# One set of the fifth group's first dense product as seven block products, with its casts moved

## The chip, the cores and the metric

The kernel runs on one core of a Trainium2 chip. The metric is the device time of one execution in microseconds (us), as the median of several runs. TensorE (PE) does matrix products and accumulates them in PSUM, a memory of banks that VectorE (DVE) and ScalarE (ACT) read. DVE, ACT and GpSimd (POOL) do the elementwise work, and SyncE (SP) issues the transfers. Each engine works through its own instructions in order and waits for others by semaphores.

## The reference

Two operators in a row: an attention with decay over blocks of 64 tokens, and a dense layer, gelu and dense layer on its result.

```python
for b in range(nb):                         # blocks of 64 tokens, 4 batches, 8 heads, 768 tokens, 64 wide
    intra = (qb @ kb^T * Dmask) @ vb        # inside the block
    inter = (qb * lam_pow) @ kv_state       # from all blocks before
    out[:, :, sl] = intra + inter
    kv_state = lam_block * kv_state + (kb * rev_pow)^T @ vb
x = out as 3072 tokens x 512
h = x @ w_in                                # 512 -> 2048, the first dense product
g = 0.5 * h * (1 + tanh(c * (h + 0.044715 * h**3)))
y = g @ w_out                               # 2048 -> 512
```

The types on the chip are float16 for the factors and float32 for the sums.

## The kernel before

The attention goes in 24 steps (0 to 23): 256 tokens of one batch, four of the eight heads. For each step the query is scaled and cast by DVE, the key cast by ACT, the value scaled by POOL, and query and key are transposed by a DMA:

```python
def cast_qk(s):
    q32, k32, _ = ld32[s]
    tqk = a16p.tile([P, 2, 2, HH, D], FP16, tag="qk16", name=f"qk16_{s}")
    tq, tk = tqk[:, 0], tqk[:, 1]
    q_eng = nc.gpsimd if s == 3 else nc.vector
    pin(q_eng.tensor_tensor(wide(tq), q32[:], decay(dq, s), ALU.mult))
    ...
    pin(nc.scalar.activation(out=wide(tk), in_=k32[:], func=AF.Copy))
```

The loaded q32, k32 and v32 lie in pools of four buffers each. Two steps' attention products are issued together as a "burst": four banks for the scores S, two for O, two for K, out of one pool of eight PSUM banks:

```python
def burst(ns, ss, *mix):
    for n in ns:
        scores(n)                                        # S: 2 banks each
    O = [ps_M.tile(..., name=f"O{c}") for c in range(2)]
    ...                                                  # O += PT x v
    if ns:
        K = [ps_M.tile(..., name=f"K{c}") for c in range(2)]
    ...                                                  # K = k^T v, then O += u x q
    for n in ns:
        causal(n)                                        # DVE: PT = S * mask, frees S
    for i, s in enumerate(ss):
        x_out(s, ...)                                    # ACT: O to xT
    ...
    for n in ns:
        update(n, 0)                                     # DVE, POOL: state from K
```

The dense layers go by groups of steps; a group's matmuls are small pieces in a queue, from which `fill(n)` takes n. In groups 0 to 4 the first product is made of pieces `mm1` (four matmuls of 512 columns, then a gelu by ACT):

```python
groups = [[0, 1], [2], [3], [4, 5], [6, 7], [8, 9], [10, 11]]
def mm1(fs):
    Hps = ps_M.tile([P, per, N], FP32, tag="M", name="Hps")
    for i, f in enumerate(fs):
        for c in range(NC):
            pin(nc.tensor.matmul(by_block(Hps[:, i, :]), w_in16[:, c, f * P : (f + 1) * P],
                                 x(c), start=(c == 0), stop=(c == NC - 1)))
    ...
    pin(nc.scalar.activation(out=dst, in_=Hps[:], func=AF.Gelu_apprx_tanh))
```

In groups 5 and 6 (`SEVEN`) it is done by Strassen-Winograd's seven products of 2x2 blocks in place of eight: four sums of x blocks (`sum_x`, tile xs) and four sums of weight blocks (`sum_win`, tiles ws), and for each set k the products m = 1 to 7, each four matmuls of 256 columns, accumulated in three banks HX, HW and HY:

```python
def seven(m, k):
    ...
    if m == 1:
        copied("m1", "q32", nc.scalar)      # ACT copies HX to a buffer of the q32 pool
    elif m == 2:
        added(0, 0, "m1")                   # DVE: m1 += HW, then a gelu by ACT
    elif m == 5:
        copied("q", "q32", nc.scalar)       # ACT copies HY
        release()                           # issues the gelus that are pending
    elif m == 6:
        copied("u2", "k32", nc.vector)      # DVE copies HX to a buffer of the k32 pool
    elif m == 3:
        added(0, 1, "u2")                   # DVE: u2 += HY
    elif m == 7:
        added(1, 1, "q")                    # DVE: q += HX
    elif m == 4:
        pending.insert(0, lambda: gelu(1, 0, dst[:]))
    if k == HF // 2 - 1 and m in (3, 7, 4):
        release()
```

m6, m7 and m4 accumulate on HX behind m1, and m3 on HY behind m5. The second dense product (banks MX, MW, MY) is done by seven block products in all groups but the first; `behind(k, ...)` attaches its DVE sums over gelu results (`sum_g`, tile gs) to the k-th piece of the group. The part of the program in question:

```python
    R(17, 15)                                # queues group 4
    fill(1); U(17); fill(1)
    sum_win(3, 0, nc.vector); fill(2)
    prep(19)
    sum_win(3, 1, nc.vector); fill(2)
    sum_win(4, 0, nc.vector); fill(2)
    sum_win(4, 1, nc.vector); fill(2)
    prep_qk(20); fill(1)
    prep_qk(21); prep_v(20); fill(3)
    burst((18, 19), (16, 17))
    prep_v(21); fill(2)
    U(18); U(19); fill(4)
    prep_qk(22); fill(2)
    burst((20, 21), (18, 19), 11, 4)         # queues group 5
    ...
```

Of the kernel before, what the change touches and what calls it, by code (L numbers as in the profile page):

```python
# [15 lines left out]
def kernel(  # L16
# [10 lines left out]
    nc = tc.nc  # L27
# [116 lines left out]
    def sum_win(m, j, eng):  # L144

        if not wi_sum:
            wi_sum.extend(wst.tile([P, 2, 2, DFF // 2], FP16, tag=f"w{2 + i}", name=f"ws{i}")
                          for i in range(2))
        a, op, b = I_SUMS[m]
        cs, fs = slice(0, 2), slice(512 * j, 512 * j + 512)  # L150
        pin(eng.tensor_tensor(w_in_block(m, cs, fs), w_in_block(a, cs, fs),
                              w_in_block(b, cs, fs), op))
# [17 lines left out]
    def load_ahead(s):  # L170
        if s < NSTEP:
            load_step(s)
# [76 lines left out]
    def wide(t):  # L249
        return t.rearrange("p j h d -> p h j d")  # L250

    def decay(t, s):
        hs = halves[s % 2]
        return t[:, hs, :].unsqueeze(3).to_broadcast([P, HH, 2, D])

    def prep_v(s):
        scale_v(s)
        if s >= 6:
            if s + 3 == FIRST_DMA_T + 1:
                load_step(s + 3, "qk")  # L260
            else:
                load_ahead(s + 3)
# [6 lines left out]
    def prep_qk(s):  # L269
        cast_qk(s)  # L270
        transpose_dma(s)

    def cast_qk(s):
        q32, k32, _ = ld32[s]
        tqk = a16p.tile([P, 2, 2, HH, D], FP16, tag="qk16", name=f"qk16_{s}")
        tq, tk = tqk[:, 0], tqk[:, 1]
        q_eng = nc.gpsimd if s == 3 else nc.vector
        pin(q_eng.tensor_tensor(wide(tq), q32[:], decay(dq, s), ALU.mult))  # L278
        if s == 0:
            inverse(halves[0])  # L280
            odd(halves[1])
            inverse(halves[1])
        pin(nc.scalar.activation(out=wide(tk), in_=k32[:], func=AF.Copy))  # L283
        a16[s] = (tq, tk)
        whole_qk[s] = tqk

    whole_qk = {}

    def transpose_dma(s):
        tqk = whole_qk.pop(s)  # L290
        if s >= FIRST_DMA_T:
            o = qkp.tile([P, 2, 2, 2, P], FP16, tag="qkT", name=f"qkT_{s}")
            pin(nc.sync.dma_start_transpose(out=o[:].rearrange("p a j h t -> p (a j h) t"),
                                            in_=tqk[:].rearrange("p a j h d -> p (a j h d)")))
            qkT[s] = o
            if s == FIRST_DMA_T:
                load_step(s + 1, "v")
# [219 lines left out]
        return gs_kept[1:]  # L517

    SEVEN = (5, 6)
    SLOTS = {5: {1: 0, 2: 1, 5: 1, 6: 1, 3: 1, 7: 1}, 4: {1: 0, 2: 1, 5: 0, 6: 1, 3: 1, 7: 1}}  # L520
    groups = [[0, 1], [2], [3], [4, 5], [6, 7], [8, 9], [10, 11]]
    group_of = {sb: (g, i) for g, sbs in enumerate(groups) for i, sb in enumerate(sbs)}
# [2 lines left out]
    def queue_group(g, lead=0, per_set=0):  # L525
# [69 lines left out]
        def product(m, p, part=None):  # L595

            st = of_group

            def bank(name):
                if name not in st:  # L600
                    st[name] = ps_M.tile([P, 1 if name == "X" else NP, HE], FP32, tag="M",
                                         name="M" + name[0])
                return st[name]

            if m in (2, 5, 3):
                dst = bank("Y" if m in (5, 3) else "W")[:, p]
            else:
                dst = bank(f"X{p}")[:, 0]
            opens = m == 1 or (m in (2, 5) and p == 0)
            closes = m in (2, 3, 4)  # L610
            a, b = FACTORS[m]
            for i in range(HF) if part is None else range(HF // 2 * part, HF // 2 * part + HF // 2):
                lhsT = g_rows(a, i)[:, p * P : p * P + P]
                if b in W_SUMS:
                    rhs = w_sum16[:, w_slot[b], i, :]
                else:
                    F, E = b
                    rhs = w_out16[:, F * HF + i, E * HE : E * HE + HE]
                pin(nc.tensor.matmul(dst, lhsT, rhs, start=(opens and i == 0),  # L619
                                     stop=(closes and i == HF - 1), skip_group_check=True))  # L620
            if part == 0:
                return
            last = p == NP - 1

            def temp(name):
                if name not in st:
                    st[name] = mtp.tile([P, NP, HE], FP32, tag=name, name=name)
                return st[name]

            def out_tile(T):  # L630
                if f"o{T}" not in st:
                    st[f"o{T}"] = otp.tile([P, NP, 2, HE], FP32, tag="o32", name=f"o{T}")
                return st[f"o{T}"]

            def copy(to, of):
                pin(nc.scalar.activation(out=to, in_=of, func=AF.Copy))  # L636

            def store(T, ps=slice(0, NP), es=slice(0, 2)):
                r = row0 + T * HN
                rows = out[r : r + HN, :].rearrange("(p q) (e d) -> q p e d", q=P, e=2)  # L640
                whole = g == 3
                for i in [ps] if whole else [slice(i, i + 1) for i in range(ps.start, ps.stop)]:
                    pin(nc.sync.dma_start(out=rows[:, i, es], in_=out_tile(T)[:, i, es, :]))

            one = slice(p, p + 1)
            if m == 1:
                copy(temp("m1")[:, p], dst)
            elif m == 2 and last:
                pin(nc.vector.tensor_tensor(out_tile(0)[:, :, 0, :], st["W"][:], st["m1"][:], ALU.add))
            elif m == 5 and last:  # L650
                copy(temp("q")[:], st["Y"][:])
            elif m == 6:
                copy(temp("u2")[:, p], dst)
            elif m == 3 and last:
                pin(nc.vector.tensor_tensor(out_tile(0)[:, :, 1, :], st["Y"][:], st["u2"][:], ALU.add))
                store(0)
            elif m == 7 and last_group:
                pin(nc.vector.tensor_tensor(out_tile(1)[:, p, 1, :], dst, st["q"][:, p], ALU.add))
                if last:
                    store(1, one, slice(1, 2))  # L660
            elif m == 7:
                copy(temp("u3")[:, p], dst)
                if last:
                    pin(nc.gpsimd.tensor_tensor(out_tile(1)[:, :, 1, :], st["u3"][:], st["q"][:],  # L664
                                                ALU.add))
            elif m == 4:
                copy(out_tile(1)[:, p, 0, :], dst)
                if last_group:
                    store(1, one, slice(0, 1 if last else 2))
                elif last:  # L670
                    store(1)
# [26 lines left out]
        def seven(m, k):  # L698
# [48 lines left out]
                added(1, 1, "q")  # L747
            elif m == 4:
                pending.insert(0, lambda: gelu(1, 0, dst[:]))
            if k == HF // 2 - 1 and m in (3, 7, 4):  # L750
                release()

        def merge(lead, per_set):
# [71 lines left out]
        def behind(k, i0, i1, ms):  # L825

            piece = filler[at + k]

            def both():
                piece()  # L830
                sum_g(i0, i1, ms)

            filler[at + k] = both
# [3 lines left out]
        if g in SEVEN:  # L837
# [6 lines left out]
            for k, m in enumerate((2, 4, 3)):  # L844
                behind(len(parts) * k, 4, 8, (m,))
            return
        for i in range(HF):
            for fs in ([[i, i + HF]] if per == 2 else [[i], [i + HF]]):
                filler.append(lambda fs=fs: mm1(fs))
        for m, p in order:  # L850
# [4 lines left out]
        if per == 2:  # L855
            behind(5, 0, 4, (1, 2))
            behind(6, 0, 4, (4, 3))
            behind(7, 4, 8, (1,))
            behind(8, 4, 8, (2,))
            behind(9, 4, 8, (4,))  # L860
            behind(10, 4, 8, (3,))
        else:
            behind(9, 0, 4, (1, 2) if g == 3 else (1, 2, 4, 3))
            if g == 3:
                behind(12, 0, 4, (4, 3))
            w = 2 if g + 1 in SEVEN else 1
            for k, m in zip((0, 3, 7, 11) if w == 2 else (0, 1, 2, 4), (1, 2, 4, 3)):
                behind(n1 + k, 4, 8, (m,))

    def fill(n):  # L870
        for _ in range(min(n, len(filler))):
            filler.pop(0)()
# [162 lines left out]
    U(17)  # L1035
    fill(1)
    sum_win(3, 0, nc.vector)
    fill(2)
    prep(19)
    sum_win(3, 1, nc.vector)  # L1040
    fill(2)
    sum_win(4, 0, nc.vector)
    fill(2)
    sum_win(4, 1, nc.vector)
    fill(2)
    prep_qk(20)
    fill(1)
    prep_qk(21)
    prep_v(20)
    fill(3)  # L1050

    burst((18, 19), (16, 17))
    prep_v(21)
    fill(2)
    U(18)
    U(19)
    fill(4)
    prep_qk(22)
    fill(2)
    burst((20, 21), (18, 19), 11, 4)  # L1060
    fill(3)
    U(20)
    U(21)
    fill(20)
    prep_qk(23)
    fill(23)
    prep_v(22)
    prep_v(23)
    fill(13)
# [34 lines left out]
```

## Time and profile before

| | |
|---|---|
| time, median of 3 runs | 199.9 us (199.7 to 201.04) |
| span of the profiled execution | 198.0 us |
| all first products Hps, 288 matmuls (L542) | 50.8 us |
| block products HX, HW, HY of groups 5 and 6, one matmul | 272 to 273 ns by the page |
| query cast on DVE, 23 times | 19.7 us, mean 859 ns |
| key cast on ACT, 24 times | 15.0 us, mean 626 ns |
| ACT waiting for Hps before its gelu | 8.8 us in 32 waits |
| POOL waiting for ACT's u before the addition o | 37.9 us in 5 waits |

The mean of a matmul on the page includes its way through the pipeline, so that neighbours overlap; how long a run of matmuls holds PE is better read from the chain of waits, where each piece is counted from the end of the one before. "Idle before" on an engine that is not on that chain costs nothing by itself. A line such as L542 is a line of the kernel before.

### The profile page before, as it was taken

Reading aid. Unit: us, or ns where it says so; the run is one execution under the profiler, and the core shown is the slowest. Engines: PE = TensorE matmul, PEld = TensorE weight load, DVE = VectorE, ACT = ScalarE, POOL = GpSimd, SP = SyncE. Lnnn points to the kernel's source line nnn. Section 1 sums busy time; section 2 is a strip of 40 time slices with the busy share of each in tenths; the row PEclk is TensorE's granted clock in tenths of the full one; section 3 lists DMA queues with packets and bytes.
Section 4 is the critical chain, followed back from the end, with each engine's and each line's share of the span. In section 5 each row is a group of like instructions: output and inputs, shape, how many; then the busy total and the mean of one; then the engine's idle time right before and its main releaser. Section 6 shows DMA issues by size and latency. Waiting matters only on the chain.

```text
span 198.0 us, 5937 instructions
## 1 busy us (share of the span) xinstructions
PE 191.6 (97%) x2439; PEld 140.2 (71%) x2439; DVE 153.9 (78%) x296; ACT 123.0 (62%) x251; POOL 75.5 (38%) x85
## 2 busy tenths in 40 slices
PE   8979999999999999999999999999999999999993
PEld 2546544456888888754588854578888888888882
DVE  4887722789999989969999927998778996588620
ACT  3673878457794675677645377844768836779221
POOL 6594213457557642465563526156002030002000
DMA  6999999999999999989994997400211200030205
GB/s 168 291 323 386 386 387 387 293 289 301 336 263 265 218 307 226 194 252 190 295 205 95 272 316 182 104 16 0 53 66 43 104 10 0 0 107 2 106 14 201
DMA packets 61722, 37.86 MB, mean 191 GB/s; under 512 B 17536, under 2 KB 54656, under 8 KB 61696
## 3 DMA queue, kind: packets, MB, share of 16 engines
q1 hardware_dynamic: 61152, 37.23, 72.9%
q8 instruction: 19, 0.31, 0.7%
q10 hardware_dynamic: 544, 0.26, 0.5%
q14 instruction: 7, 0.06, 0.1%
HBM read 27.26 MB, written 6.29 MB: 169 GB/s over the span
## 4 chain that ended last, share of the span: by engine, by line
PE 88%; SPq 4%; DMA 4%; ACT 1%; issue 1%
PE Hps L542 24%; PE MX L619 17%; PE MY L619 9%; PE HX L711 7%; PE O2ps L557 7%; PE MW L619 4%; DMA wi<-in_moe_w_in_dram 4%; SPq L70 4%; PE HY L711 4%; PE S L340 3%; PE Hps L802 3%; PE HW L711 2%; PE OK L398 2%; PE O L449 1%; PE O L424 1%; PE Tps L311 1%
## 5 line engine op out<-in xcount | busy, mean ns | idle before, releaser
L542 PE MATMUL Hps<-xT,w_in 128*128 128x512 f16 (+1 forms) x288 | 50.8, 332 | 0.0
L501 POOL TENSOR_TENSOR u<-t,lumask 128x256 f16<-128x256 f32 x40 | 31.0, 789 | 46.5 <-DVE t L494 28.4
L542 PEld LDWEIGHTS <-w_in 128*128 128x128 f16 x288 | 27.8, 98 | 19.0
L546 ACT ACTIVATE gT<-Hps 128x512 f16<-128x512 f32 x56 | 33.1, 598 | 9.3 <-PE Hps L542 8.8
L350 DVE TENSOR_TENSOR PT<-S,mask 128x512 f16<-128x512 f32 x48 | 30.3, 681 | 6.5 <-PE S L340 6.4
L619 PEld LDWEIGHTS <-gs 128*128 128x128 f16 x320 | 31.2, 98 | 3.6
L266 POOL TENSOR_TENSOR v<-v,dv 128x512 f16<-128x512 f32 x24 | 30.0, 1254 | 7.4 <-DMA v<-in_v_dram 7.2
L619 PEld LDWEIGHTS <-gT 128*128 128x128 f16 x240 | 23.2, 98 | 3.6 <-ACT gT L546 0.5
L619 PE MATMUL MX<-w_sum,gs 128*128 128x256 f16 x160 | 21.4, 273 | 0.0
L664 POOL TENSOR_TENSOR o<-u,q 128x512 f32<-128x512 f32 (+1 forms) x5 | 5.8, 1158 | 37.9 <-ACT u L636 37.9
L278 DVE TENSOR_TENSOR qk<-q,dq 128x512 f16<-128x512 f32 x23 | 19.7, 859 | 0.6 <-DMA q<-in_q_dram 0.5
L283 ACT ACTIVATE qk<-k 128x512 f16<-128x512 f32 x24 | 15.0, 626 | 6.5 <-DMA k<-in_k_dram 6.4
L589 DVE TENSOR_TENSOR gs<-gT 128x1024 f16<-128x1024 f16 (+1 forms) x24 | 17.6, 737 | 1.5 <-ACT gT L546 1.5
L557 PE MATMUL O2ps<-w_out,gT 128*128 128x512 f16 x64 | 14.6, 379 | 0.0
L475 ACT ACTIVATE xT<-OK 128x256 f16<-128x256 f32 x26 | 10.0, 453 | 7.3 <-PE OK L398 7.1
L711 PEld LDWEIGHTS <-ws 128*128 128x128 f16 x128 | 12.5, 98 | 1.8
L636 ACT ACTIVATE u<-MX 128x256 f32<-128x256 f32 x18 | 6.9, 384 | 10.2 <-PE MX L619 10.2
L475 ACT ACTIVATE xT<-O 128x256 f16<-128x256 f32 x22 | 8.0, 459 | 5.9 <-PE O L449 5.0
L557 PEld LDWEIGHTS <-gT 128*128 128x128 f16 x64 | 6.1, 98 | 6.6
L619 PE MATMUL MY<-w_out,gs 128*128 128x256 f16 x80 | 10.7, 273 | 0.0
L340 PEld LDWEIGHTS <-qkT 64*64 64x64 f16 x384 | 6.0, 106 | 6.5 <-issue 2.5
L589 DVE TENSOR_TENSOR gs<-gs,gT 128x1024 f16<-128x1024 f16 (+1 forms) x12 | 10.2, 851 | 0.3
(95 smaller groups left out, 319.4 us busy)
## 6 DMA issues: line engine op xcount, KB each, us to landing
q<-in_q_dram SPq DMA_DIRECT2D x24, 256.0 KB, 5.0
k<-in_k_dram SPq DMA_DIRECT2D x24, 256.0 KB, 5.2
v<-in_v_dram SPq DMA_DIRECT2D x23, 256.0 KB, 5.4
out_dram<-o SPq DMA_DIRECT2D x19, 256.0 KB, 4.3
wo<-in_moe_w_out_dram SPq DMA_DIRECT2D x4, 1024.0 KB, 9.5
wi<-in_moe_w_in_dram SPq DMA_DIRECT2D x4, 512.0 KB, 7.0
wi<-in_moe_w_in_dram SPq DMA_DIRECT2D x2, 1024.0 KB, 12.8
out_dram<-o SPq DMA_DIRECT2D x2, 512.0 KB, 6.6
```

The lines of the kernel that those rows point to most:

```text
L266: pin(nc.gpsimd.tensor_tensor(wide(tv[:]), ld32[s][2][:], decay(dv, s), ALU.mult))
L278: pin(q_eng.tensor_tensor(wide(tq), q32[:], decay(dq, s), ALU.mult))
L283: pin(nc.scalar.activation(out=wide(tk), in_=k32[:], func=AF.Copy))
L350: pin(nc.vector.tensor_tensor(t[:, hl].rearrange("p b c d -> p b (c d)"), Sps[:].rearrange("p b c d -> p b (c d)"), mask[:].unsqueeze(1).t ...
L475: pin(nc.scalar.activation(out=d, in_=o, func=AF.Copy))
L501: pin(nc.gpsimd.tensor_tensor(u[:], state[half][:].unsqueeze(2).to_broadcast([P, 2, 2, D]), lumask[:, 2 * half : 2 * half + 2, :].unsqueez ...
L542: pin(nc.tensor.matmul(by_block(Hps[:, i, :]), w_in16[:, c, f * P : (f + 1) * P], x(c), start=(c == 0), stop=(c == NC - 1)))
L546: pin(nc.scalar.activation(out=dst, in_=Hps[:], func=AF.Gelu_apprx_tanh))
L557: pin(nc.tensor.matmul(O2[tau][0][:], gT[:, f % HF, f // HF, tau * P : (tau + 1) * P], w_out16[:, f, :], start=(n == 0), stop=(n == NF - 1)))
L589: pin(nc.vector.tensor_tensor(g_rows(m, i), g_rows(a, i), g_rows(b, i), op))
L619: pin(nc.tensor.matmul(dst, lhsT, rhs, start=(opens and i == 0), stop=(closes and i == HF - 1), skip_group_check=True))
L711: pin(nc.tensor.matmul(dst[:, i, :], w_in_block(a, slice(c, c + 1), slice(f * P, f * P + P))[:, 0], x_block(b, slice(c, c + 1))[:, 0], sta ...
```

## The change

Group 4, the fifth, gets one of its sets (k = 0: rows 0, 1, 8 and 9 of sixteen) by the seven block products; the other twelve pieces stay as they were. It is meant to take matmul columns off PE: seven products of 4 x 256 columns for four pieces of 4 x 512. The group's four x sums are made ahead of it. Because the products' temporaries take buffers of the q32 and k32 pools, which here still carry loaded steps, the key casts of 20 and 21 are issued earlier, the load of 23 comes after the burst, and the casts of 22 and 23 come within the sixth group. The group's second store is issued in two halves.

```diff
+    def cast_q(s):
+        both16(s)
+        q_eng = nc.gpsimd if s == 3 else nc.vector
+        pin(q_eng.tensor_tensor(wide(a16[s][0]), ld32[s][0][:], decay(dq, s), ALU.mult))
+
+    def cast_k(s):
+        both16(s)
+        pin(nc.scalar.activation(out=wide(a16[s][1]), in_=ld32[s][1][:], func=AF.Copy))
...
+    MIXED = 4
...
-                whole = g == 3
+                whole = g == 3 and T == 0
...
-            if k == HF // 2 - 1 and m in (3, 7, 4):
+            if (k == HF // 2 - 1 or g == MIXED) and m in (3, 7, 4):
                 release()
...
-        for i in range(HF):
+        if g == MIXED:
+            sum_xs.append(sum_x)
+            plain = [[f] for i in range(2, HF) for f in (i, i + HF)]
+            for m in (1, 2, 5, 0, 6, 3, 0, 7, 0, 4):
+                filler.append((lambda m=m: seven(m, 0)) if m else (lambda fs=plain.pop(0): mm1(fs)))
+            for fs in plain:
+                filler.append(lambda fs=fs: mm1(fs))
+        for i in range(HF) if g != MIXED else ():
...
-            behind(9, 0, 4, (1, 2) if g == 3 else (1, 2, 4, 3))
+            n1 += 3 * (g == MIXED)
+            behind(n1 - 7, 0, 4, (1, 2) if g == 3 else (1, 2, 4, 3))
...
     sum_win(3, 0, nc.vector)
+    cast_k(20)
     fill(2)
     prep(19)
...
     fill(2)
+    cast_k(21)
     sum_win(4, 1, nc.vector)
-    fill(2)
-    prep_qk(20)
-    fill(1)
-    prep_qk(21)
-    prep_v(20)
+    for m in (1, 2, 3, 4):
+        sum_xs[0](m)
+    cast_q(20)
+    transpose_dma(20)
+    scale_v(20)
     fill(3)
+    cast_q(21)
+    fill(7)

     burst((18, 19), (16, 17))
+    transpose_dma(21)
+    load_ahead(23)
     prep_v(21)
-    fill(2)
+    fill(3)
     U(18)
     U(19)
-    fill(4)
-    prep_qk(22)
-    fill(2)
+    fill(3)
     burst((20, 21), (18, 19), 11, 4)
     fill(3)
     U(20)
     U(21)
     fill(20)
+    prep_qk(22)
+    fill(12)
     prep_qk(23)
-    fill(23)
+    fill(11)
     prep_v(22)
```

More of the change, by code (lines that the diff above doesn't have):

```diff
@@ L273, in cast_qk @@
     def cast_qk(s):
[L274 to L278, printed above, removed]
+        cast_q(s)
         if s == 0:
@@ L282, in cast_qk, with both16 @@
             inverse(halves[1])
-        pin(nc.scalar.activation(out=wide(tk), in_=k32[:], func=AF.Copy))
-        a16[s] = (tq, tk)
-        whole_qk[s] = tqk
+        cast_k(s)
+    def both16(s):
+        if s in a16:
+            return
+        tqk = a16p.tile([P, 2, 2, HH, D], FP16, tag="qk16", name=f"qk16_{s}")
+        a16[s] = (tqk[:, 0], tqk[:, 1])
+        whole_qk[s] = tqk
+    def cast_q(s):
[5 more added lines that the diff above has]
+        pin(nc.scalar.activation(out=wide(a16[s][1]), in_=ld32[s][1][:], func=AF.Copy))
     whole_qk = {}
@@ L519 @@
     SEVEN = (5, 6)
+    MIXED = 4
+    sum_xs = []
     SLOTS = {5: {1: 0, 2: 1, 5: 1, 6: 1, 3: 1, 7: 1}, 4: {1: 0, 2: 1, 5: 0, 6: 1, 3: 1, 7: 1}}
```

## The prediction

> **What bounds the kernel now.** I read the busy shares first, then the chain that ended last, then the order of time on each engine around 113 us, where the changed piece runs. The page's first line of numbers and the chain's share by engine:
>
> ```profile
> PE 191.6 (97%) x2439; PEld 140.2 (71%) x2439; DVE 153.9 (78%) x296; ACT 123.0 (62%) x251; POOL 75.5 (38%) x85
> PE 88%; SPq 4%; DMA 4%; ACT 1%; issue 1%
> ```
>
> TensorE (PE) is busy nearly always and carries 88% of the chain; the rest of it is the first loads and the last store. So a matmul cycle saved shortens the run, and any wait PE is made to take lengthens it: nothing later has slack to take it back. The chain in order of time (start, us, what), around the fifth group (steps 12 to 15, group 4 in the code) and in the sixth group's first set:
>
> ```profile
> 112.95 4.32 PE Hps L542 x20
> 117.26 0.57 PE S L340 x32
> 119.09 6.91 PE Hps L542 x32
> 125.99 0.57 PE S L340 x32
> ...
> 136.32 0.44 PE HY L711 x4
> 136.76 0.44 PE HX L711 x4
> 137.19 0.44 PE MX L619 x4
> 137.63 0.52 PE HY L711 x4
> ```
>
> Four 512-column matmuls take 4.32 / 5 = 0.864 us (one Hps piece); four of 256 columns take 0.437 us. The 0.52 of the last line is a 0.08 us wait: HY must wait until ScalarE has copied that bank. The copy ran 136.91 to 137.50, so PE restarts about 0.2 us after the end of the record it waits for. I use that 0.2 below.
>
> Now VectorE (DVE), GpSimd (POOL) and ScalarE (ACT) in order of time at the start of the group (start, us, engine, instruction, idle before):
>
> ```profile
> 111.70 2.35 DVE L278 TENSOR_TENSOR qk<-q,dq 128x512 f16<-128x512 f32 x2
> 117.66 2.48 DVE L350 TENSOR_TENSOR PT<-S,mask 128x512 f16<-128x512 f32 x4 [3.60 <-PE S L340]
> ...
> 111.70 1.81 POOL L664 TENSOR_TENSOR o<-u,q 128x512 f32<-128x512 f32 x1 [2.27 <-ACT u L636]
> 113.47 1.49 POOL L266 TENSOR_TENSOR v<-v,dv 128x512 f16<-128x512 f32 x1
> ...
> 112.98 0.38 ACT L636 ACTIVATE o<-MX 128x256 f32<-128x256 f32 x1 [0.49 <-PE MX L619]
> 113.85 0.60 ACT L546 ACTIVATE gT<-Hps 128x512 f16<-128x512 f32 x1 [0.48 <-PE Hps L542]
> ```
>
> DVE does the query casts of 20 and 21, then idles 3.6 us. The change puts its additions into that hole. But the two casts took 2.35 us where one elsewhere takes 0.68, and just then POOL has two operations.
>
> **What the Trainium skill says.** "SBUF — State Buffer", section "SBUF: two separate sides": a VectorE operation with two SBUF inputs and a GpSimd operation that reads SBUF share a port pair, as an exclusive lock held for the whole instruction. The trace agrees: the first cast ran 111.70 to 112.38; the second is recorded as 112.30 to 114.05 (1.75 us), ending 0.54 after POOL's o addition (111.70 to 113.51), and POOL's v scaling (113.47, 1.49 us) ends 0.9 us after that cast. Where nothing stands against them, the same o addition takes 1.27 (at 151.35) and the v scaling 1.04 (at 121.56). They take turns, one instruction each; 107 to 110 us shows the same turns. "TensorE: Matmul & The Clock Gate", "Back-to-back issue gap", gives 518 cycles for 512 columns and 262 for 256, that is, hardly any fixed cost for halving a matmul; 0.864 against 0.437 agrees. "PSUM — Partial Sum Buffer", "PSUM: the matmul accumulator": eight banks. All eight are in one pool here, and a burst takes eight (four S, two O, two K).
>
> **The change part by part.**
> *Matmul work.* Of the 16 Hps pieces four go (4 x 0.864 = 3.46 us); seven block products come (7 x 0.437 = 3.06). PE: **-0.40 us**. This is all that can be gained directly.
>
> *The schedule if nothing waits*, from 112.95, products by their number m: m1 to 113.39, m2 113.82, m5 114.26, Hps 115.13, m6 115.57, m3 116.00, Hps 116.87, m7 117.31, Hps 118.18, then the burst; m4 after it.
>
> *Wait A, m3.* m3 accumulates on the bank of m5, so ACT must first have copied it (0.60). That copy's buffer is the fourth-oldest of the query buffers, the one of step 20, so it waits for the query cast of 20 on DVE. Ahead of that cast now stand the four x sums, each with two SBUF inputs. DVE ends its weight sums at 111.78 as before. In turns with POOL: first x sum to 112.1, POOL o (1.27) to 113.35, second x sum to 113.7, POOL v (1.04) to 114.7, third and fourth x sum (0.34 apart without contention, at 163.16 and 163.50) to 115.4, cast (0.6) to 116.0. ACT copy to 116.65, PE at 116.85 instead of 115.57: **+1.28 us**. Were there no turns, the cast would end near 113.7 and nothing would wait.
>
> *Wait B, the burst's K bank.* HX stays occupied across the burst until m4, so seven banks serve eight tiles. In the compiled program K0 takes the bank of the third Hps and so waits for its gelu; K1 takes the bank of the burst's own first S and waits for its masking. From wait A: m3 ends 117.29, m7 118.59, third Hps 119.46, S and O (0.57 + 0.45) 120.48. DVE's addition for m7 runs 118.63 to 119.32; ACT, in order, does the gelu of it and then that of the third Hps (about 0.52 and 0.60 after a start near 119.66): 120.78, PE at 120.98. **+0.5 us.** K1's masking ends near 120.54, under this.
>
> *Wait C, second burst.* It comes 7.1 us after the first instead of 8.73 (five Hps and m4 between them, not eight Hps). The four sums over gelu results ended 8.5 us after the first burst's start before; they still depend on the first Hps after the burst, and the masking of the next S stands behind them, so the next Hps, which needs that bank, waits some 0.3. The query cast of 22, moved away from there, gives no relief to the sums themselves. **+0.3 us.**
>
> *Moved or hidden.* The key casts of 20 and 21 (0.62 each) go into ACT gaps (1.78 us idle before 110.42); key 21 was issued at 107.38 and lands in 4.0 us, before 112.4 where it is wanted. Four more DVE operations of 0.69 fit the 3.6 us hole. In the sixth group the casts of 22 and 23 take the place of cast 23 and a gap of 0.86. The 512 KB store split in two costs one more issue (about 0.8) on a queue that is not on the chain. One wait of 0.06 us before the third burst (154.37, 0.50 instead of 0.44) goes, since m4 there now comes behind the burst: **-0.06**.
>
> Sum: -0.40 - 0.06 + 1.28 + 0.5 + 0.3 = **+1.6 us**, as the full working has it.
>
> **The rivals.**
> *All waits hide.* If DVE keeps the port for its run of x sums, cast 20 ends by 114.7, m3 does not wait, and the rest is 0.2 to 0.4 us of wait B. For it: DVE won the port at 111.70 although POOL was ready. Against: at 101 to 103.5 and 107 to 110 us they took strict turns. Time: 199.4 to 199.9.
> *The transposed loads become the bound.* Transpose 21 waits for the first burst's last product with step 16; before, it was issued at 118.9 and landed 3.1 us later, and its scores were wanted at 126.3. Now it is issued 1 to 2.5 us later and wanted at about the same time: some 2 us of slack remain. If a store stood ahead of it in the queues it could cost 1 to 2 us: 201 to 202.
> *ScalarE becomes tight in the sixth group* with both key casts among its copies and gelus; K0 of the third burst waits for ACT's o copy, which in the trace before ends at 155.60, 0.3 us before K was wanted. Up to +0.5.
>
> **Range and chances.** The mechanism of A and B is read from the program's own waits, but each is a difference of two long chains that I know to some 0.4 us, and waits overlap rather than add where one delays both sides. I therefore take a little more than half of the sum: 199.9 + 0.9 = **200.8 us**. Low end 199.4: everything hides. High end 201.9: all waits and a bit of another. Two per cent is 4 us; nothing in sight is that large: faster 0.01, same 0.96, slower 0.03.
>
> **What would show it.** Right, by step: 16 Hps pieces become 12, with 28 more matmuls of 256 columns at 109 ns; in the chain, a product HY near 115.6 to 117 that takes visibly more than 0.44, released by ACT's copy, and behind that the cast of q; a second wait at K in the first burst, released by ACT's gelu; DVE's x sums at 111.7 to 115.5 in turns with POOL. Wrong: cast 20 ending before 114.7 (A is gone), K not waiting (B is gone), or a wait at the scores of 20 and 21 for a transpose. The prediction is also wrong if POOL's o addition moves, for the whole of A hangs on its coinciding with the x sums.

## The result, and the profile after

The changed kernel takes **202.71 us** (median; 202.63 to 203.13), the kernel before it 199.87 us beside it: ratio **1.0139, 95% interval 1.0111 to 1.0167**. It is slower by 2.8 us, where the prediction said 0.9 with a high end of 2.0. The span of the profiled execution goes from 198.0 to 201.0 us.

From the page of the changed kernel, the busy times and then the engines' shares of the chain of waits:

```profile
PE 192.5 (96%) x2451; PEld 141.9 (71%) x2451; DVE 159.8 (80%) x304; ACT 123.7 (62%) x253; POOL 74.7 (37%) x85
...
PE 70%; DVE 11%; ACT 7%; SPq 4%; DMA 4%; issue 2%; DVEq 0%
```

Before, TensorE held 88% of the chain and DVE had no share that was listed. Now DVE holds 11% and ACT 7%: in places PE waits for ACT, and ACT for DVE. The busy time of PE does not show the saved 0.40 us (it even rises by 0.9, and by 0.3 in a second profile of the same kernel); the positions below do.

Where PE lost its time is read from its timeline in the changed kernel. Columns: start in us, us from the first to the last of the row, engine, line, operation, out<-in, shape, count, and in brackets the idle time and who ended it.

```profile
114.95 0.60 PE L723 MATMUL HX<-xs,ws 128*128 128x256 f16 x4
116.36 0.60 PE L723 MATMUL HY<-xT,ws 128*128 128x256 f16 x4 [0.81 <-ACT q L734]
119.52 0.62 PE L434 MATMUL O<-PT,v 64*64 64x128 f16 x32
120.46 0.45 PE L448 MATMUL K<-v,qk 64*64 64x64 f16 x32 [0.33 <-ACT gT L558]
128.30 3.61 PE L554 MATMUL Hps<-xT,w_in 128*128 128x512 f16 x16 [0.46 <-DVE PT L360]
157.35 0.44 PE L448 MATMUL K<-v,qk 64*64 64x64 f16 x16 [0.16 <-ACT o L648]
183.53 0.60 PE L631 MATMUL MX<-w_sum,gT 128*128 128x256 f16 x4 [0.41 <-ACT u L648]
```

The bracket counts from the modelled end of the matmul before it and so tells less than PE loses. What PE loses is the start less the start that steady work would give. m6 (the first row) starts at 114.95, a product takes 0.44, so m3 (the second row) was due at 115.39: **A = 0.97**. The O products start at 119.52 and take 0.45, so K was due at 119.97: **B = 0.49**. Hps behind the second burst was due at 127.68: **C = 0.62**. K of the third burst was due at 156.91 (**0.44**) and the MX of the last group at 182.96 (**0.57**). The kernel before has no wait of 0.1 us or more in any of these places.

The group's first matmul starts at 112.77 (112.78 before), its second product MX at 131.75 (130.05 before). That is +1.70, and 0.97 + 0.49 + 0.62 - 0.40 make 1.68. The last MX ends 2.53 later than before.

The DVE timeline of the changed kernel at the group's start:

```profile
111.69 0.41 DVE L702 TENSOR_TENSOR xs<-xT 128x512 f16<-128x512 f16 x1
112.13 1.38 DVE L702 TENSOR_TENSOR xs<-xT,xs 128x512 f16<-128x512 f16 x1
113.43 1.26 DVE L702 TENSOR_TENSOR xs<-xT 128x512 f16<-128x512 f16 x1
114.61 0.41 DVE L702 TENSOR_TENSOR xs<-xT,xs 128x512 f16<-128x512 f16 x1
114.95 0.68 DVE L291 TENSOR_TENSOR qk<-q,dq 128x512 f16<-128x512 f32 x1
```

The POOL timeline of the same stretch:

```profile
111.69 1.54 POOL L676 TENSOR_TENSOR o<-u,q 128x512 f32<-128x512 f32 x1 [2.27 <-ACT u L648]
113.19 1.22 POOL L266 TENSOR_TENSOR v<-v,dv 128x512 f16<-128x512 f32 x1
```

And the ACT timeline:

```profile
115.71 0.60 ACT L734 ACTIVATE q<-HY 128x512 f32<-128x512 f32 x1 [1.71 <-DVE qk L291]
118.29 0.63 ACT L740 ACTIVATE gT<-u 128x512 f16<-128x512 f32 x1 [0.91 <-DVE u L744]
119.82 0.59 ACT L558 ACTIVATE gT<-Hps 128x512 f16<-128x512 f32 x1
```

The three are one story. Two of the four x sums take 0.41 us. The second ends 0.28 us after POOL's o addition (113.51 against 113.23), the third 0.28 us after POOL's v scaling (114.69 against 114.41). So the query cast of 20 ends at 115.63, ACT's copy q<-HY can only then start, and m3 behind it. Then ACT waits for DVE's u addition before a gelu, and the gelu of the third Hps, three places further in ACT's row, ends at 120.41; K's bank comes free with it.

The busy times from 112.80 to 130.00 us, first in the kernel before, then in the changed one. Columns: window, its length, then busy time (count) of PE, weight load, DVE, ACT and POOL, the granted clock, the DMA share and GB/s.

```profile
112.80:130.00 17.20, 17.20 (x270) 9.25 (x268) 12.48 (x25) 13.15 (x27) 6.99 (x9) 1.00 0.86 195
```

```profile
112.80:130.00 17.20, 15.60 (x274) 9.69 (x272) 15.86 (x28) 11.72 (x25) 5.83 (x7) 1.00 0.83 183
```

In these 17.2 us DVE goes from 12.5 to 15.9 us busy. PE gained 0.40 us of work and DVE was given 3.4 us more in the same window, in which it already had to mask two bursts and sum four gelu results. These are records and not work alone: the two long x sums hold turns with POOL, as the query cast of 21 did before (1.75 us where a cast elsewhere takes 0.68).

### The profile page after: what moved, and what is told of

Its sections match the earlier page's. It is cut to its first block, busy times and chain, and to the rows that moved or that the text cites. A ratio compares the mean times of both kernels' runs of the same rounds, so it can differ in the third digit from the quotient of the medians.

```text
span 201.0 us, 5974 instructions
## 1 busy us (share of the span) xinstructions
PE 192.5 (96%) x2451; PEld 141.9 (71%) x2451; DVE 159.8 (80%) x304; ACT 123.7 (62%) x253; POOL 74.7 (37%) x85
## 4 chain that ended last, share of the span: by engine, by line
PE 70%; DVE 11%; ACT 7%; SPq 4%; DMA 4%; issue 2%; DVEq 0%
PE Hps L554 19%; PE MX L631 12%; PE MY L631 7%; PE O2ps L569 7%; PE HX L723 5%; PE MW L631 4%; DMA wi<-in_moe_w_in_dram 4%; SPq L70 4%; ACT gT L740 3%; PE Hps L814 3%; DVE gs L601 3%; PE HY L723 2%; PE S L350 2%; PE OK L408 1%; DVE ws L151 1%
## 5 line engine op out<-in xcount | busy, mean ns | idle before, releaser
L554 PE MATMUL Hps<-xT,w_in 128*128 128x512 f16 (+1 forms) x272 | 47.7, 329 | 0.5 <-DVE PT L360 0.5
L554 PEld LDWEIGHTS <-w_in 128*128 128x128 f16 x272 | 26.3, 98 | 17.4 <-issue 0.6
L558 ACT ACTIVATE gT<-Hps 128x512 f16<-128x512 f32 x52 | 30.7, 597 | 9.1 <-PE Hps L554 8.8
L266 POOL TENSOR_TENSOR v<-v,dv 128x512 f16<-128x512 f32 x24 | 29.3, 1224 | 8.1 <-DMA v<-in_v_dram 6.5
L601 DVE TENSOR_TENSOR gs<-gT 128x1024 f16<-128x1024 f16 (+1 forms) x24 | 19.5, 815 | 1.1 <-ACT gT L558 1.1
L291 DVE TENSOR_TENSOR qk<-q,dq 128x512 f16<-128x512 f32 x23 | 18.8, 816 | 0.6 <-DMA q<-in_q_dram 0.6
L723 PEld LDWEIGHTS <-ws 128*128 128x128 f16 x144 | 14.0, 98 | 3.3 <-issue 1.0
L723 PEld LDWEIGHTS <-w_in 128*128 128x128 f16 x108 | 10.5, 98 | 1.2
L631 PE MATMUL MX<-w_sum,gT 128*128 128x256 f16 x80 | 10.5, 273 | 0.4 <-ACT u L648 0.4
L723 PE MATMUL HX<-xs,ws 128*128 128x256 f16 x72 | 10.8, 273 | 0.0
```

Of the source, the lines that this page charges most:

```text
L266: pin(nc.gpsimd.tensor_tensor(wide(tv[:]), ld32[s][2][:], decay(dv, s), ALU.mult))
L291: pin(q_eng.tensor_tensor(wide(a16[s][0]), ld32[s][0][:], decay(dq, s), ALU.mult))
L601: pin(nc.vector.tensor_tensor(g_rows(m, i), g_rows(a, i), g_rows(b, i), op))
L723: pin(nc.tensor.matmul(dst[:, i, :], w_in_block(a, slice(c, c + 1), slice(f * P, f * P + P))[:, 0], x_block(b, slice(c, c + 1))[:, 0], sta ...
```

## The experiments

The start of the group differs between profiled executions (112.68 to 113.84 us; see the last section). The medians of the table were taken beside runs of the kernel before that lay between 199.58 and 199.97. Besides the median, each kernel is read by two distances in its profile that do not hold this: from the group's first matmul to its second product MX (which holds the two bursts), and from there to the end of the last MX. The medians of the changed kernel on two occasions, 202.71 and 203.11, differ by 0.4 us; its distances agree within 0.01.

| kernel | median us | first matmul to MX | MX to the end of the last |
|---|---|---|---|
| before | 199.87 | 17.26 | 64.65 |
| changed | 202.71 | 18.98 | 65.48 |
| moves alone | 199.69 | 17.26 | 64.62 |
| query copy in a key buffer | 202.91 | 18.86 | 65.48 |
| v of 20 early | 202.55 | 18.51 | 65.48 |
| one more Hps ahead of m7 | 203.50 | 19.23 | 65.49 |
| one more piece between the bursts | 202.03 | 18.21 | 64.62 |
| the same again | 201.81 | 18.22 | 64.63 |
| one more piece behind the second burst | 201.96 | 18.98 | 64.63 |
| all three waits eased | 199.88 | 17.58 | 64.62 |
| the same, m4 ahead of the burst | 200.01 | 17.62 | 64.62 |
| eased, cast of 21 behind the burst | 200.05 | 17.59 | 64.62 |
| m4 ahead, cast of 21 behind the burst | 200.58 | 18.10 | 64.63 |
| changed kernel again | 203.11 | 18.99 | 65.48 |

**The moves without the products.** The kernel before, with only the moved casts, the transpose of 21 and the load of 23 behind the burst, and the split store (it is the second store of the fourth group, not of the fifth).

```diff
-        pin(q_eng.tensor_tensor(wide(tq), q32[:], decay(dq, s), ALU.mult))
+        cast_q(s)          # and cast_k(s), as in the change
 ...
+    cast_k(20)             # early, as in the change
 ...
     burst((18, 19), (16, 17))
+    transpose_dma(21)
+    load_ahead(23)
```

> The kernel before with only the moves of the change: key casts of 20 and 21 early, transpose 21 and load 23 behind the burst, casts of 22 and 23 in the sixth group, the second store of the fourth group in halves; no block products in the fifth group, no x sums there. Theory 'the moves are hidden': 199.8 us, within 0.2 of before. Rival 'the casts of 22 and 23 in the sixth group delay its copies and gelus on ScalarE': 200.2 to 200.6, with a wait of K in the third burst for ScalarE's o copy as in the changed kernel.

Measured: 199.69 us, ratio 0.9988 (0.9973 to 1.0002). PE's timeline there:

```profile
112.78 4.48 PE L552 MATMUL Hps<-xT,w_in 128*128 128x512 f16 x20
...
130.05 1.91 PE L629 MATMUL MX<-w_out,gT 128*128 128x256 f16 x16
```

Both starts are those of the kernel before to the hundredth, and the third burst's K starts without a wait although the key casts stand where the change puts them. All moves are hidden; the loss belongs to the products and what they bring with them.

**Wait A: another buffer for the copy of m5.**

```diff
-                copied("q", "q32", nc.scalar)
+                copied("q", "k32" if g == MIXED else "q32", nc.scalar)
```

> ScalarE's copy of HY goes to a buffer of the key pool (step 20's, whose cast is done at 107.8) and no longer waits for the query cast of step 20 (which ends at 115.63 in the changed kernel). Theory 'the buffer' (the copy's buffer alone makes the 0.97 us wait of m3): m3 starts near 115.4 instead of 116.36, and the time falls by 0.8 to 1.0 us, to about 201.8. Rival 'VectorE is late anyway': VectorE's own row of work (x sums, cast 20, m1 addition, cast 21) is unchanged, so its copy of HX still ends at 117.4 and m7 starts at 117.66 as now; the wait moves from m3 to m7 and the time stays within 0.2 us of 202.7.

Measured: 202.91 us, ratio 1.0141 (1.0111 to 1.0172). PE's timeline:

```profile
116.22 0.60 PE L723 MATMUL HY<-xT,ws 128*128 128x256 f16 x4
...
118.39 0.60 PE L723 MATMUL HX<-xs,ws 128*128 128x256 f16 x4 [0.70 <-DVE u L736]
```

m3 no longer waits, but m7 does, 0.86 us, for DVE's copy of m6 to u. That copy stands in DVE's row behind the same x sums and casts. The path to MX shortens by 0.12, not by 0.97. So the buffer is only the place where the lateness of DVE shows; take it away and the next product that needs DVE waits.

**Wait A: POOL's v scaling out of the x sums' way.**

```diff
     prep(19)
+    scale_v(20)
 ...
     transpose_dma(20)
-    scale_v(20)
```

> GpSimd's scaling of v of step 20 is issued ahead of its o addition, in its idle time near 109.4 to 111.7, so one GpSimd operation fewer stands against VectorE's x sums. Theory 'turns at the port': the third x sum no longer takes 1.26 us but 0.41, cast 20 ends near 114.8 instead of 115.63, m3 waits 0.2 us instead of 0.97, and the time falls by 0.5 to 0.8 us, to about 202.0. Rival 'the x sums are slow of themselves or wait for their inputs': the third sum stays at 1.2 us and the time stays at 202.7.

Measured: 202.55 us, ratio 1.0135 (1.0116 to 1.0154). DVE's timeline:

```profile
111.91 1.49 DVE L702 TENSOR_TENSOR xs<-xT 128x512 f16<-128x512 f16 x1
113.43 0.43 DVE L702 TENSOR_TENSOR xs<-xT,xs 128x512 f16<-128x512 f16 x1
113.77 0.42 DVE L702 TENSOR_TENSOR xs<-xT 128x512 f16<-128x512 f16 x1
114.44 0.69 DVE L291 TENSOR_TENSOR qk<-q,dq 128x512 f16<-128x512 f32 x1
```

Only one x sum is now long, the one that meets POOL's o addition (which here started first, at 111.66). The third fell from 1.26 to 0.42 us. The cast stands 0.5 us earlier, m3 starts 0.94 after m6 instead of 1.41, and the path to MX is shorter by 0.47. So a turn with POOL is worth about half of wait A, as the prediction had it; the other turn was left in place. The median, at 202.55, shows only 0.16 of this, less than the 0.5 to 0.8 expected: behind the last MX the profile is 0.32 longer than that of the changed kernel.

**Wait B: what K waits for.** One Hps piece is drawn ahead of m7, so that K gets another bank.

```diff
-            for m in (1, 2, 5, 0, 6, 3, 0, 7, 0, 4):
+            for m in (1, 2, 5, 0, 6, 3, 0, 0, 7, 4):
```

> The third Hps piece is put ahead of m7, so that its gelu no longer stands behind the gelu that needs VectorE's addition for m7, and K0's bank comes free some 1 us earlier. Theory 'the gelu of the third Hps' (it alone holds up K): the 0.49 us wait in the first burst goes, the time falls by 0.4 to 0.5 us, to 202.3. Rival 'K1 waits for the masking of the burst's own S, which ends at 120.2': the wait shrinks from 0.49 to 0.4 us, and the time stays at 202.6 to 202.7.

Measured: 203.50 us, ratio 1.0194 (1.0155 to 1.0234). PE's timeline:

```profile
119.90 0.19 PE L448 MATMUL K<-v,qk 64*64 64x64 f16 x1
120.44 0.44 PE L448 MATMUL K<-v,qk 64*64 64x64 f16 x31 [0.34 <-DVE PT L360]
```

The first matmul of K starts without a wait; the rest waits for the masking PT of the burst's own scores. Both reasons of wait B are there, and taking away the first leaves the second. Besides, the wait at 128 grew (the bracket from 0.46 to 0.67), and the path to MX by 0.25. The median rose by 0.79, which neither expectation allowed for; its four times spread from 202.89 to 204.42, and beyond the 0.25 on the path and 0.29 behind the last MX the rise is not explained.

**Wait C and the later waits: the queue shifted by one piece.** The change puts 19 pieces in place of 16 into the group's queue, but draws only two more of them up to the second burst (9 and 6, where it was 5 and 8). So four pieces are left behind that burst instead of three, and all that comes later is one piece off against the bursts. First one more Hps is drawn between the two bursts:

```diff
     U(18)
     U(19)
-    fill(3)
+    fill(4)
     burst((20, 21), (18, 19), 11, 4)
```

> One more piece of the queue is issued ahead of the second burst, so that three pieces are left behind it as in the kernel before, and m4 of the sixth group's last set comes ahead of the third burst again. Theory 'one piece of shift': the 0.6 us wait behind the second burst, the 0.4 us wait of K in the third burst and the 0.6 us wait in the last group all go, and the time falls by 1.2 to 1.6 us, to about 201.3. Rival 'the waits come from the moved casts or the added work and not from the shift': they reappear at their places, and the time falls by 0.3 us at most.

Measured: 202.03 us, ratio 1.0111 (1.0092 to 1.0129). PE's timeline:

```profile
129.46 2.75 PE L554 MATMUL Hps<-xT,w_in 128*128 128x512 f16 x12
...
157.71 0.42 PE L448 MATMUL K<-v,qk 64*64 64x64 f16 x16
```

Neither row has a bracket any more: wait C is gone, and K of the third burst finds its bank free; MX of the last group does too. The distances fall by 0.77 and 0.85. Of the 0.77, wait C is 0.62; wait A too was some 0.14 shorter in both profiles of this kernel, for a reason that was not sought. But the median fell by 0.68 only, so this kernel was measured once more beside the changed one:

> The kernel with one more piece between the bursts (m4 ahead of the second one) once more, beside the changed kernel on the same chip. From the group's start to the last MX its profile was 1.62 us shorter than the changed kernel's, its median only 0.68. Theory (that profiled execution began the group 1.07 late because of its first loads, and few runs were timed): a second profile again shows 82.7 to 83.0 us from the group's start, with the group's start anywhere from 112.7 to 113.8, and the median is 201.3 to 201.7. Rival (the piece sets something earlier or at the end that takes the gain back): the median stays at 202.0, as that of the kernel with one more piece behind the second burst, and the part before the group or behind the last MX is longer again.

> The changed kernel as it is, beside the run before it. Expected: 202.6 to 202.8; from the group's start to the last MX 84.4 to 84.5 us, as both its profile and the kernel with the other query buffer show; the rival of the run before expects nothing else of this one.

Measured: 201.81 us (ratio 1.0117, 1.0094 to 1.0140) against 203.11 (1.0178, 1.0157 to 1.0200), a difference of 1.30. Both distances repeat within 0.01, so the gain of 1.6 on the path is there; this kernel starts the group 0.2 later than the changed one (112.92 and 112.70), and its median lies above the 201.7 that was expected at most, as that of the changed kernel lies above 202.8.

To part wait C from the two later waits, the piece is drawn behind the second burst instead:

```diff
     burst((20, 21), (18, 19), 11, 4)
-    fill(3)
+    fill(4)
```

> The changed kernel with one more piece drawn from the queue behind the second burst (four instead of three), nothing else: all that comes later stands again against the bursts and the attention's pieces as in the kernel before, while the three waits around the first two bursts stay. Theory (the two late waits, K of the third burst for ScalarE's o copy and MX of the last group for its u copy, come from the shift of the queue by one piece): group's start to its second product stays at 18.98 us, both late waits are gone, the wait of 0.07 at m4 ahead of the third burst comes back, and from the group's start to the last MX it is 83.5 us instead of 84.47; the time is 201.8. Rival (they come from VectorE and ScalarE being 1.7 us later since the first bursts, whatever the order): both stay, 84.4 and 202.7.

Measured: 201.96 us, ratio 1.0093 (1.0065 to 1.0122). PE's timeline:

```profile
157.31 0.42 PE L448 MATMUL K<-v,qk 64*64 64x64 f16 x16
...
183.89 1.91 PE L631 MATMUL MX<-w_out,gT 128*128 128x256 f16 x16
```

The path to MX stays at 18.98 with all three waits A, B and C, and the rest falls from 65.48 to 64.63, that of the kernel before. So the late waits do not follow from DVE and ACT being 1.7 us late at the first bursts. They come from the order alone: m4 of the sixth group's last set stands behind the third burst, and the last group is interleaved one piece off.

**All waits eased at once.** The key buffer, the early v of 20, the fourth piece between the bursts, and the cast of 21 three pieces later. Only the last of these edits is new:

```diff
     cast_q(20)
     transpose_dma(20)
     fill(3)
+    fill(3)
     cast_q(21)
-    fill(7)
+    fill(4)
```

> Four edits of the changed kernel together: v of step 20 scaled early (as in the run before), HY's copy in a key buffer, the query cast of 21 behind VectorE's copy of HX, and one more piece ahead of the second burst. Theory 'VectorE's row of work sets m3 and m7, the one piece of shift sets the later waits, and the burst's eighth bank is left': m3 and m7 start without a wait, and of all waits only that of K in the first burst (0.4 to 0.5 us) stays. Against the kernel before: -0.40 -0.06 +0.45, so 199.8 us, the same as before within 0.2. Rival 'HX, HY and HW cost more than matmul time in other ways as well': it stays 0.5 us or more above before.

Measured: 199.88 us, ratio 0.9998 (0.9988 to 1.0008). One wait is left in PE's timeline:

```profile
120.30 0.45 PE L448 MATMUL K<-v,qk 64*64 64x64 f16 x32 [0.37 <-ACT gT L558]
```

K was due at 119.60, so it costs 0.70, and 0.70 less the 0.40 saved is the 0.31 by which the path to MX is longer than before. The cast of 21 now stands right ahead of DVE's addition for u, ACT waits 0.8 us for that addition, and the gelu of the third Hps comes after it. The rest of the loss is gone: wait A was DVE's lateness, C went with the piece that gives DVE 0.86 us more ahead of the second burst, the later waits with the order of the queue; what stays is a part of B. That K waits 0.70, and not the 0.4 to 0.5 expected, and the median still equals that of the kernel before is partly luck: the path is 0.29 longer to the last MX and the part behind it 0.10 shorter.

**m4 ahead of the burst**, so that no bank is held: `fill(5)` for `fill(4)` in the last diff, and `fill(2)` behind the burst.

> As e5, but m4 comes ahead of the first burst, so that HX's bank is free for it and no K has to wait for the masking of the burst's own S; one piece fewer behind the burst. Theory 'a bank held across the burst is the rest of the loss': m4 itself waits 0.1 us for VectorE's addition, K1 0.1 to 0.2 us for m4's gelu; against the kernel before -0.40 -0.06 +0.3, so 199.6 us. Rival 'ScalarE's row of gelus, which K waits for in both, is the bound': K waits as long as in e5 or longer, 199.9 to 200.3.

Measured: 200.01 us, ratio 1.0009 (0.9997 to 1.0022). PE's timeline:

```profile
120.72 0.21 PE L448 MATMUL K<-v,qk 64*64 64x64 f16 x1
121.20 0.44 PE L448 MATMUL K<-v,qk 64*64 64x64 f16 x31 [0.27 <-ACT gT L740]
```

K's first matmul is only 0.1 us late, the others wait for the gelu of m4's own HX, which ends ACT's row of gelus. The wait has moved from the bank to ACT, as the rival had it.

**The cast of 21 behind the burst.** The last attempt to get under the kernel before, in both versions:

```diff
-    cast_q(21)
     fill(4)                # fill(5) with m4 ahead
     burst((18, 19), (16, 17))
+    cast_q(21)
     transpose_dma(21)
```

> The kernel of the run before it with all three waits eased (own buffer for the query, v of 20 early, one more fill), and the query cast of 21 moved from ahead of the first burst to right behind it. Theory (the K bank waits for two things: first for ScalarE's gelu of the third Hps, which stands behind the gelu of the block products and so behind VectorE's cast and additions; and, 0.3 us earlier, for the masking of the burst's own scores): with the cast out of the way K in the first burst waits some 0.3 us instead of 0.70, the products still save 0.40 and the wait at 154.37 0.06, so MX of the group starts 16.9 us after the group's first product (17.27 before, 17.58 in the run with the cast ahead) and the time is 199.5. Rival (the cast only changes its place): the gelu sums behind the burst come 0.6 us later on VectorE, the masking of the next burst with them, and Hps behind the second burst waits that much: K waits 0.3, Hps 0.3 to 0.6, and the time stays at 199.9 to 200.1. Second rival: the transposed load of 21, 4 us later, becomes what the scores of 20 and 21 wait for: over 200.5.

> The same move of the query cast of 21 in the kernel whose last product m4 stands ahead of the first burst. Theory that ScalarE's row of four gelus and copies ahead of K is what K waits for there: nothing of that row waits for the cast, K still waits 0.5 and the time is 199.9 to 200.1. Rival that the cast also delayed that row through VectorE's additions: m4's wait of 0.14 goes, K waits 0.2, and the time is 199.6.

Measured: 200.05 us, ratio 1.0008 (0.9997 to 1.0020), and 200.58, ratio 1.0042 (1.0021 to 1.0062). PE's timeline in the first of them, then in the second:

```profile
120.03 0.45 PE L448 MATMUL K<-v,qk 64*64 64x64 f16 x32
...
128.50 2.75 PE L554 MATMUL Hps<-xT,w_in 128*128 128x512 f16 x12 [0.23 <-DVE PT L360]
```

```profile
128.69 2.75 PE L554 MATMUL Hps<-xT,w_in 128*128 128x512 f16 x12 [0.61 <-DVE PT L360]
```

In the first, K is 0.32 late instead of 0.70 as the theory asked, but Hps behind the second burst is now some 0.4 late, and the path to MX is 17.59 against 17.58. The rival is right: the cast only changed its place. In the second, K's wait and m4's shrank as well and Hps lost more than both gained: 200.58 lies above what either expectation said. Behind the burst the cast takes 1.12 us instead of 0.68, beside POOL's u, and the gelu sums and the masking stand behind it. So in the first version it costs PE the same ahead of the burst or behind it. None of the versions with the products beats the kernel before.

## Why the prediction was wrong

The time lies 0.8 us above the high end of the range. By its steps:

*Matmul work, -0.40*: right. With the three waits as measured, the +1.70 of the path to MX adds up only with it.

*Wait A, +1.28*: the mechanism right, as the early v showed for one of its two turns; the size 0.97. Each turn was a little shorter than in the working: POOL's o ended at 113.23 (113.35 there), its v at 114.41 (114.7), and so the cast of 20 at 115.63 (116.0). What the working did not have is that the buffer of the copy hardly matters: with another one, m7 waits for DVE instead.

*Wait B, +0.5*: right, 0.49, for the reason named, and the masking as the floor under it was right too.

*Wait C, +0.3*: right in kind (the gelu sums stand ahead of the masking, and the second burst came 7.09 us after the first), 0.62 in size. The working left it as an estimate, without following DVE's row. The first gelu sum before, then the same sum and POOL's scaling of v in the changed kernel:

```profile
122.34 0.80 DVE L589 TENSOR_TENSOR gs<-gT 128x1024 f16<-128x1024 f16 x1 [1.05 <-ACT gT L546]
```

```profile
123.73 1.27 DVE L601 TENSOR_TENSOR gs<-gT 128x1024 f16<-128x1024 f16 x1 [0.58 <-ACT gT L558]
123.41 1.04 POOL L266 TENSOR_TENSOR v<-v,dv 128x512 f16<-128x512 f32 x1
```

The sum starts 1.39 us later, after waiting for ACT's gelu, itself late from wait B, and takes 0.47 longer. It runs beside POOL's scaling, a meeting of the two engines that the working did not have; where the sum came first (m4 ahead of the burst) it took 0.69 and the scaling 1.52. The sums and the masking run without a gap from there. No run moved this scaling alone.

*The sum of these, +1.6*: 1.70 to 1.71 by the path to MX.

*"I therefore take a little more than half of the sum"*: **this step failed first**. The reason given was that waits overlap rather than add. They do overlap in the sense that easing one lets another out, as the buffer, the other Hps and the moved cast all showed. But that argument is for taking a wait away. When all of them stand, one after the other on the path of PE, they add, and here they added to within 0.1 us: 1.70 was measured where 0.9 was booked. The full sum would have given 201.5, which is still inside the range; the missing term carries the time out of it.

*The term that was missing*: the late waits. The one at the third burst's K was named as a rival, "up to +0.5", with ACT as the releaser; it measured 0.44. Its cause as the prediction put it, key casts that make ACT tight in the sixth group, is not what was found: with one piece more it is gone, and the moves alone, with the same casts, have no such wait. The prediction had seen that m4 would come behind the third burst, but booked from it only the -0.06 (0.07 measured). The same move took away the time in which ACT made its copy. Before:

```profile
153.34 1.04 PE L619 MATMUL MX<-w_sum,gT 128*128 128x256 f16 x8
154.28 0.60 PE L711 MATMUL HX<-xs,w_in 128*128 128x256 f16 x4
154.81 0.64 PE L340 MATMUL S<-qkT 64*64 64x128 f16 x32
155.21 0.39 ACT L636 ACTIVATE o<-MX 128x256 f32<-128x256 f32 x1
155.72 0.42 PE L438 MATMUL K<-v,qk 64*64 64x64 f16 x16
```

Changed:

```profile
155.03 1.04 PE L631 MATMUL MX<-w_sum,gT 128*128 128x256 f16 x8
156.00 0.64 PE L350 MATMUL S<-qkT 64*64 64x128 f16 x32
156.91 0.39 ACT L648 ACTIVATE o<-MX 128x256 f32<-128x256 f32 x1
```

The copy ends 2.26 to 2.27 us after MX starts in both. Without m4 (the HX row) between them, S follows MX after 0.97 us instead of 1.47, so K is wanted 0.50 sooner, and the copy, which ended 0.12 ahead of K, now ends 0.39 after the time K was due. The 0.3 us of margin in the prediction counts K from the end of the matmul before it; less 0.50 it was already used up.

The wait at the last group's MX, 0.57, was not foreseen at all; the kernel with one more piece behind the second burst shows it to come from the same shift. Together, less some small waits that went, the late waits are 65.48 - 64.65 = 0.83 us.

1.70 and 0.83 make 2.53 of the 2.84 us between the medians. The rest is about what the tail differs by in the profiles (below).

*The transposed loads as the bound*: did not happen. The transpose of 21, issued later, hides in the kernel with the moves alone and in the changed one.

*The Trainium skill*, "SBUF — State Buffer", section "SBUF: two separate sides", carried wait A. The changed kernel agrees with its exclusive lock for a whole instruction: an x sum of 0.41 us alone takes 1.38 and 1.26 us where POOL's o and v run, and in the kernel with the early v it is the first sum that takes 1.49, because there POOL came first.

## What to carry to other kernels

Before work is moved off the engine that bounds, add up what the new form gives to the other engines **in the same stretch**: here 0.40 us of matmul time was bought with 3.4 us more of DVE time in 17 us that had 4.7 to spare, turns with POOL included. Where an engine has no slack, waits that lie one after the other on its path are added in full; that removing one brings little does not mean that having all costs little. And a change in the length of a queue shifts everything that is drawn from it later: count the pieces at every later burst, and give back the missing one.

## What was not expected of the hardware

Two things, both left open. First, the time from the end of the last MX to the end of the span is 3.15 to 3.28 us in the profiles of the kernel before, of the moves alone and of the five kernels with the query copy in a key buffer, and 3.73 to 4.16 us in the other seven, the changed one (3.73 and 4.16) among them. The last store takes 1.7 us from issue to landing in the five of the former whose landing is recorded, 2.3 to 2.7 in the latter. The changed kernel and the one with the key buffer have the same instructions in the same order on each engine and differ in a buffer alone. The 0.45 by which the two first profiles differ would cover the 0.31 us that the path leaves of the medians' difference, but the median of the kernel with the key buffer is no lower. Its profile began the group 0.84 us later than the changed kernel's, and three of its four executions took 202.9, the fourth 201.78; so a gain at the end may be hidden by the second effect. Why a buffer used 80 us earlier should matter to a store was not tried.

Second, the start of the group lies between 112.68 and 113.84 us in kernels with nearly the same instructions up to there. In four profiles (starts 112.92, 113.39, 113.50 and 113.84) PE waits 0.3 to 0.5 us, until 94.8 to 95.7, for a transposed load; in both of the changed kernel there is no such wait. The kernel with one more piece between the bursts had it in both its profiles, with starts of 113.84 and 112.92. Its cause was not found.
